# First products of four token quads at 512 tokens wide, in an attention and feed-forward kernel on one core

## The chip, the cores and the metric

The kernel runs on one core of a Trainium2 chip. The metric is device time in microseconds for one execution. The engines are TensorE (PE, with PEld for its weight loads), VectorE (DVE), ScalarE (ACT), GpSimd (POOL) and SyncE (SP). The last two mostly issue DMAs here.

## The reference

A gated recurrent attention over 4 batches, 8 heads, 768 tokens and 48 values a head is followed by a feed-forward layer of width 2048 on the 3072 tokens of 384 values. Cut to what matters:

```
for t in range(S):
    new_re = ar * S_re - ai * S_im
    new_im = ar * S_im + ai * S_re
    S_re, S_im = new_re + k[t] v[t]^T, new_im
    y[t] = q[t] S_re
x = y as (3072, 384)
h = x @ w_in
out = (h * sigmoid(h)) @ w_out
```

## The kernel before, in words

**Tiling.** The tokens are cut into 24 chunks of 128 (number n) and 12 pairs of chunks, 256 tokens each (number p). A chunk goes through gates, a phase and a decay (cumulative sums done as products with a triangle, tiles `phase` and `L`, lines 462 and 465), sine and cosine, rotated keys and queries (`kr`, `qr`), the weights `a` of the attention (line 609), their mask (`w`, line 620) and the output `y` (lines 639 and 642, for the first chunks 671 and 674). `put` (step x, lines 683 and 687) copies `y` from PSUM to `xT`; the last 16 values of three pairs of heads take a DMA (`third_of`, step xd, line 651).

**Feed-forward.** The first product makes 2048 hidden units in eight steps jp of 2 x 128 units. `hidden` (step h) writes one PSUM tile of 128 x 512 for pair p and step jp: two units blocks (ji) times 256 tokens. For the pairs 0 and 1 it is a plain float32 product (line 761). For the pairs from 2 on it is a sum of three float32r products: `xT` is split by `x_head`, `x_tail` and `x_diff` (steps xh, xt, xg) into the forms `xH` (ACT, line 778), `xL` (DVE, line 858) and `xD` (DVE, line 862), 128 x 768 each, and `w_in` into a head, a tail (`fine`, loaded again by DMA) and a difference (`mixed`). `sums` runs 3 forms x 3 parts of the 384 inputs x 2 units blocks = 18 products with 128 x 128 stationary weights and 256 moving tokens (line 768). `silu` (step g, line 312) makes `g`; `g_rounded`, `g_tail` and `g_diff` (steps gr, gb, gc; ACT line 914, DVE lines 858 and 862) split it into `head`, `tail` and `gd`, one buffer each; `result_of_parts` (step r, line 953) adds 12 products of 384 columns to the two PSUM tiles `o` of the pair. After eight steps `copied` (step oc, line 966) takes them out.

**Quads.** From pair 2 on, two neighbouring pairs (2 and 3, 4 and 5, and so on) share the loaded weights: the steps h, g, gr, gb, gc and r of an even pair p and of p + 1 stand close to each other for the same jp. Each pair has its own `xH`, `xL`, `xD`, in tiles with the tags of p % 2, so the forms of pair p + 2 wait only for the last product of pair p.

**Order.** The order of all instructions is written out by hand as a table of 1899 steps under `manual_schedule`: every engine runs its own instructions in the order in which the steps name them. The step `warm` puts idle products (bf16, 256 columns, line 990) on PE. The special functions of ACT lie in several tables; a step that needs another table than the loaded one puts an ACT_TABLE_LOAD in front (line 306).

Of the kernel before, what the change touches and what calls it, by code (L numbers as in the profile page):

```python
# [70 lines left out]
def kernel(  # L71
# [854 lines left out]
    def result(p, jp):  # L926
        if "o" not in A[p]:
            A[p]["o"] = o_tiles(p, 2)
# [3 lines left out]
        for m in range(2):  # L932
            for ji in range(2):
# [143 lines left out]
    with tc.manual_schedule():  # L1077
        for x in """
                re:0 im:0 e0:0 re:1g e1:0 e2:0 q:0g e3:0 im:2g im:1 e4:0 e0:1 hold: e1:1 re:2g e6:0
                e2:1 im:3g re:3g e5:0 k:0g F: v:0g e7:0 e4:1 e8:0 e6:1 F: L:0 e3:1 exp:0 e7:1 e8:1  # L1080
# [3 lines left out]
                R: dk:1 G8:1 G4:1 T:0.1 G6:1 ends:0 warm:20 T:0.2 G9:1 v:1g sm:0 H: q:2g lk:0 F:
                trig:1 dq:1 lk:1 last:0 T:0.0 F: J: v:2g Ga:1 s:0 rq:1.1 re:4g w:0.0 rk:1.1 R: L:2
                L:3 H: R: thirds:0 re:5g phase:2 S:0 t:1.1 rq:1.0 im:4g J: w:0.1 im:5g exp:2 rk:1.0
                k:3g ends:1 exp:3 t:1.2 m:0.0 rd:2 R: F: turn:2 t:1.0 trig:2 T:1.1 m:0.1 t:1.3 dk:2
                last:2 T:1.0 T:1.2 y:0 dq:2 T:1.3 phase:3 q:3g rd:3 thirds:1 rq:2.0 w:1.0 t:2.2
                ends:2 H: rq:2.1 x:0 J: w:1.1 G0:2 rk:2.0 turn:3 trig:3 dk:3 m:1.0 t:2.0 rk:2.1
                G5:2 dq:3 F: s:1 t:2.3 m:1.1 q:4g H: F: F: T:2.3 v:4g S:1 thirds:2 rk:3.1 G8:2 y:1  # L1090
                k:4g R: T:2.2 J: t:2.1 s:2 ends:3 rq:3.1 G1:2 last:3 thirds:3 x:1 rq:3.0 rk:3.0
                G7:2 t:3.1 J: T:2.0 H: R: S:2 h:0.0 H: G2:2 T:2.1 H: R: w:2.0 t:3.3 G3:2 m:2.0 J:
                G6:2 R: J: t:3.0 T:3.1 F: F: w:2.1 R: T:3.3 G4:2 t:3.2 G9:2 k:5g h:0.1 m:2.1 last:1
                q:5g w:3.1 H: T:3.2 T:3.0 y:2 m:3.1 R: Ga:2 x:2 im:6g w:3.0 L:4 exp:4 m:3.0 y:3 F:
                H: J: H: im:7g F: re:6g g:0.0 J: s:3 h:0.3 x:3 carried:4 dk:4 J: phase:4 R: F: S:3
                F: carried:5 R: g:0.1 H: R: h:0.2 rd:4 J: re:7g J: ends:4 turn:4 H: F: L:5 g:0.3
                r:0.0 dq:4 phase:5 k:6g h:1.1 trig:4 g:0.2 K:4 Q:4 R: tk:4 J: H: exp:5 G0:3 F:
                h:1.0 G5:3 J: G1:3 q:6g tq:4 H: last:4 F: H: v:5g G7:3 s:4 R: ends:5 F: G2:3 G8:3
                G3:3 r:0.1 J: rd:5 r:0.2 S:4 G6:3 H: G4:3 turn:5 G9:3 Ga:3 dq:5 R: g:1.0 td:4 g:1.1
                J: F: im:8g F: sm:2 last:5 H: trig:5 carried:6 dk:5 r:0.3 R: J: L:6 h:1.2 R: K:5  # L1100
                g:1.2 F: w:4.1 h:0.4 carried:7 tk:5 F: Q:5 H: J: lk:2 re:8g exp:6 H: h:1.3 R:
                phase:6 m:4.1 g:0.4 dk:6 R: rd:6 J: tq:5 R: turn:6 trig:6 phase:7 r:1.0 H: F: re:9g
                R: im:9g ends:6 s:5 r:1.1 k:7g J: last:6 rd:7 R: S:5 turn:7 H: trig:7 J: H: L:7
                w:4.0 F: m:4.0 G0:4 h:1.4 g:1.3 G5:4 h:1.5 dq:6 r:0.4 K:6 H: Q:6 R: J: g:1.4 F:
                G1:4 H: J: td:5 exp:7 q:7g R: ends:7 J: G7:4 y:4 G2:4 tk:6 tq:6 G3:4 r:1.2 G4:4
                G6:4 g:1.5 F: R: h:0.5 F: h:0.7 k:8 H: J: hl:8 R: g:0.5 H: J: J: G8:4 vh:1 vh:0
                G9:4 h:0.6 v:6g w:5.1 wq:0 x:4 vt:0 q:8 vt:1 wq:3 dq:7 td:6 wq:6 Q:7 m:5.1 dk:7
                w:5.0 s:6 r:1.3 Ga:4 ul:8 vh:2 vh:3 m:5.0 vk:0 L:8 ss:6 vk:1 q:9 k:9 wq:2 wq:4 K:7
                exp:8 y:5 carried:8 vt:2 im:10 g:0.6 vt:3 re:10 last:7 tk:7 vk:2 x:5 v:7g ht:8
                r:1.4 w:6.1 tq:7 dk:8 ut:8 w:6.0 m:6.1 carried:9 m:6.0 vk:3 phase:8 vh:4 g:0.7 vh:5  # L1110
                wq:7 ends:8 rd:8 vt:5 vt:4 td:7 turn:8 ht:9 ut:9 s:7 h:1.6 vk:5 ss:7 phase:9 h:1.7
                vh:6 vt:6 trig:8 vh:7 r:0.5 dq:8 im:11 Q:8 vk:4 hl:9 r:1.5 last:8 xd:2 wq:5 K:8
                ul:9 vk:6 y:6 vt:7 wq:1 wd:0 sd:7 rd:9 vk:7 x:6 re:11 wd:1 ws:0 wd:2 turn:9 wk:0
                w:7.0 wd:3 w:7.1 ws:2 wd:4 m:7.0 sd:6 m:7.1 G0:5 ws:4 wk:2 ws:3 y:7 tk:8 g:1.6 x:7
                wk:4 G5:5 v:8 last:9 wk:3 tq:8 L:9 g:1.7 xd:3 xh:2 wd:5 G1:5 r:1.6 xt:2 r:0.6 ws:5
                G7:5 lv:2.0 wk:5 r:0.7 r:1.7 ws:1 xg:2 G2:5 wd:6 wk:1 G3:5 wd:7 vx:2.0 ws:7 exp:9
                xh:3 xt:3 xg:3 G6:5 td:8 h:2.0 h:3.0 w:8.0 dk:9 ws:6 wk:7 s:8 lv:2.1 of:1 g:2.0
                m:8.0 wk:6 gr:2.0 G9:5 g:3.0 G8:5 w:8.1 Ga:5 vx:2.1 carried:10 re:12 of:0 gb:2.0
# [276 lines left out]
```

## Time and profile before

| what | value |
|---|---|
| median of 3 runs | 616.13 us (613.35 to 617.29) |
| profiled execution | 616.33 us |
| its span, first to last instruction | 614.5 us |
| mean granted clock of TensorE | 0.992 |
| busy: PE, DVE, ACT, POOL | 584.0, 495.9, 434.0, 222.4 us |

Durations below are from the profiled execution. It ran 1.8 us beyond its span and is within 0.2 us of the median. A matmul row of the profile lasts longer than the distance to the next one, because matmuls are pipelined; what one costs is read from start to start.

### The profile page before, as it was taken

How to read it: one execution, taken by the hardware profiler on the slowest of the kernel's cores; microseconds unless marked ns; L12 is line 12 of the kernel's file. 1: busy time of each engine (PE TensorE's matmuls, PEld its weight loads, DVE VectorE, ACT ScalarE, POOL GpSimd, SP SyncE). 2: the span in 40 equal slices, each digit the busy share in tenths (PEclk: the TensorE clock that was granted, in tenths of full speed). 3: DMA queues.
4: the chain of work that ended last, by engine and by line, in shares of the span. 5: the costliest groups of instructions: out<-in, count | busy, mean ns of one | idle time of the engine just before them, and what ended most of it. 6: DMA issues, size and time to landing. Idle time of an engine off the chain costs nothing. (4 is left out here: it accounts for less than half of the span.)

```text
span 614.5 us, 12718 instructions
## 1 busy us (share of the span) xinstructions
PE 584.0 (95%) x4404; PEld 538.2 (88%) x4404; DVE 495.9 (81%) x765; ACT 434.0 (71%) x689; POOL 222.4 (36%) x389
## 2 busy tenths in 40 slices
PE   3678999999998999999999999999999999999997
PEld 2457877777768999999999999999999999999996
DVE  5689989889988899888798989889989686566453
ACT  7789989799496798598797596897984742333222
POOL 6256343543631345533272553325640233000000
PEclk9879999999999999999999999999999999999999
DMA  9859698987778989768967768786768576664462
GB/s 180 201 136 190 184 195 189 203 160 205 202 234 244 218 163 238 161 157 186 212 159 186 154 156 225 180 187 149 177 156 255 146 186 155 203 201 136 160 201 80
DMA packets 167733, 112.30 MB, mean 183 GB/s; under 512 B 137725, under 2 KB 143425, under 8 KB 167665
## 3 DMA queue, kind: packets, MB, share of 16 engines
q1 hardware_dynamic: 151920, 89.69, 57.0%
q0 software_dynamic: 12288, 17.23, 14.0%
q10 hardware_dynamic: 3456, 4.52, 2.0%
q8 instruction: 36, 0.59, 0.4%
q14 instruction: 33, 0.26, 0.1%
HBM read 81.14 MB, written 11.47 MB: 151 GB/s over the span
## 5 line engine op out<-in xcount | busy, mean ns | idle before, releaser
L596 POOL DMA_DIRECT2D T<-sq x120 | 69.9, 590 | 67.3 <-PE h L768 24.0
L914 ACT ACTIVATE head<-g 128x512 fp32r<-128x512 f32 x75 | 47.4, 632 | 56.1 <-PE o L953 47.1
L312 ACT ACTIVATE g<-h 128x512 f32<-128x512 f32 x96 | 56.2, 593 | 40.5 <-PE h L768 34.4
L768 PE MATMUL h<-xL,fine 128*128 128x256 f32 x480 | 83.7, 283 | 0.8 <-DMA fine<-w_firsts 0.8
L768 PE MATMUL h<-xD,mixed 128*128 128x256 f32 x480 | 82.8, 280 | 1.0 <-DVE mixed L862 0.6
L306 ACT ACT_TABLE_LOAD x63 | 80.8, 1283 | 2.3 <-ACT ot L966 0.8
L858 DVE SCALAR_TENSOR_TENSOR tail<-g,head 128x512 fp32r<-128x512 f32 x75 | 51.5, 687 | 31.3 <-ACT head L914 21.6
L527 POOL DMA_DIRECT2D dec<-ends x48 | 31.3, 663 | 106.7 <-DMA ends<-eq 99.2
L768 PEld LDWEIGHTS h<-xD,mixed 128*128 128x128 f32 x480 | 68.5, 189 | 1.6 <-DVE mixed L862 1.0
L768 PEld LDWEIGHTS h<-xL,fine 128*128 128x128 f32 x480 | 68.3, 188 | 1.1 <-DMA fine<-w_firsts 1.1
L953 PE MATMUL o<-coarse,head 128*128 128x384 f32 x300 | 66.8, 344 | 0.0
L953 PE MATMUL o<-diff,gd 128*128 128x384 f32 x300 | 65.4, 339 | 0.7 <-DMA diff<-w_diffs 0.7
L768 PE MATMUL h<-xH,firsts 128*128 128x256 f32 x360 | 62.5, 282 | 0.0
L609 PE MATMUL a<-T 96*128 96x128 f32 x384 | 52.8, 285 | 3.9 <-ACT T L601 3.9
L953 PE MATMUL o<-fine,tail 128*128 128x384 f32 x260 | 55.6, 336 | 0.0
L609 PEld LDWEIGHTS a<-T 96*128 96x128 f32 x384 | 49.9, 198 | 6.5 <-ACT T L601 4.9
L953 PEld LDWEIGHTS o<-diff,gd 128*128 128x128 f32 x300 | 53.6, 188 | 1.5 <-DVE w L620 1.0
L862 DVE TENSOR_TENSOR gd<-tail,g 128x512 fp32r<-128x512 f32 x75 | 51.4, 686 | 4.2 <-PE o L953 0.2
L768 PEld LDWEIGHTS h<-xH,firsts 128*128 128x128 f32 x360 | 52.7, 188 | 0.5 <-issue 0.4
L953 PEld LDWEIGHTS o<-coarse,head 128*128 128x128 f32 x300 | 50.2, 188 | 1.5 <-issue 1.3
L728 POOL DMA_DIRECT2D S<-ssq x84 | 46.9, 607 | 12.8 <-DVE ssq L717 6.7
L953 PEld LDWEIGHTS o<-fine,tail 128*128 128x128 f32 x260 | 46.2, 188 | 0.0
(159 smaller groups left out, 1283.8 us busy)
## 6 DMA issues: line engine op xcount, KB each, us to landing
fine<-w_firsts SPq DMA_DIRECT2D x40, 384.0 KB
diff<-w_diffs SPq DMA_DIRECT2D x40, 384.0 KB
T<-sq SPq DMA_DIRECT2D x120, 64.0 KB
T<-sq POOLq DMA_DIRECT2D x120, 64.0 KB, 3.8
small<-in_moe_w_in_dram SPq DMA_DIRECT2D x16, 384.0 KB
raw<-in_moe_w_out_dram SPq DMA_DIRECT2D x16, 384.0 KB
small<-in_moe_w_out_dram SPq DMA_DIRECT2D x16, 384.0 KB
raw<-in_moe_w_in_dram SPq DMA_DIRECT2D x24, 192.0 KB
```

What stands on the lines that cost most here:

```text
L306: nc.scalar.preload_act_table_set(SETS[of][0])
L312: nc.scalar.activation(out=out, in_=in_, func=func, **kw)
L527: nc.gpsimd.dma_start(out=x["dec"][a * D:(a + 1) * D], in_=ends[n].rearrange("(h d) -> d h", d=D))
L596: (nc.gpsimd if a % 2 else nc.sync).dma_start(out=to[ts(b, Q), :, a], in_=X[n]["sq"][ts(a, Q), b].rearrange("p w h x -> p (w h) x"))
L609: nc.tensor.matmul(ps[:, h], lhsT=x["kT"][hh * HH + h], rhs=x["qT"][hh * HH + h], start=True, stop=True)
L728: (nc.gpsimd if g % 2 else nc.sync).dma_start(out=to[ts(b, Q), r, :, e], in_=sq[ts(g, Q), :, b, 0:e.stop - e.start])
L768: nc.tensor.matmul(ps[:, ji], lhsT=w(dc, ji), rhs=x[:, dc], start=(f == 0 and dc == 0), stop=(f == len(forms) - 1 and dc == ND - 1))
L858: nc.vector.scalar_tensor_tensor(out=dst, in0=whole, scalar=MORE / FINER, in1=head.bitcast(F32), op0=ALU.mult, op1=ALU.subtract)
L862: nc.vector.tensor_tensor(out=dst, in0=tail, in1=whole, op=ALU.subtract)
L914: nc.scalar.mul(g_form(p, jp, "head"), A[p]["g", jp], MORE * SPLIT / FINER)
L953: nc.tensor.matmul(to, lhsT=left[:, ji, ts(m, C)], rhs=right(ji), start=(first_ and ji == 0 and n == 0), stop=(last_ and ji == 1 and n == 2))
```

## The change: what it does

For the eight pairs 2 to 9 (`wide`), one step h no longer makes two units blocks for 256 tokens but one units block for the 512 tokens of both pairs: the step of the even pair makes block 0 of jp, that of the odd pair block 1. It is 9 products with 512 moving tokens in the place of 18 with 256. For this the forms of both pairs of a quad lie in one tile (`quad_tile`), which is written again only when the whole quad's products have been done; the pairs 10 and 11 use the same tiles but keep the narrow product. The small tiles of the start that borrow the room of the forms (`l0`, `l1`, `kr1`, `kr3`, four masks) are cut from these larger tiles.

The second product follows: `g`, `head`, `tail` and `gd` of a step now hold one units block for 512 tokens, and `result_of_quads` adds it to the four `o` tiles of both pairs. It has 12 products of 384 columns a step, as before.

The table of steps holds the same 1899 steps, the three `warm` among them, in another order.

```diff
@@ hidden
             fine, diff = (A[lead(p)][name, jp] for name in ("fine1", "mixed1"))
+            if wide(p):
+                forms = [(J[kind, lead(p)], w) for kind, w in
+                         (("xH", head_of(lead(p), jp)), ("xL", fine), ("xD", diff))]
+                for f, (x, w) in enumerate(forms):
+                    for dc in range(ND):
+                        nc.tensor.matmul(ps, lhsT=w[:, dc, ts(p % 2, C)], rhs=x[:, :, dc],
+                                         start=(f == 0 and dc == 0),
+                                         stop=(f == len(forms) - 1 and dc == ND - 1))
+                return
...
+    def wide(p):
+        return QUADS <= p < NP - 2
+
+    def quad_tile(key, i, dtype, name):
+        both = J.setdefault(key, None)
+        if both is None:
+            both = J[key] = moe.tile([C, 2, ND, T], dtype, tag=key[0], name=name, bufs=1)
+        return both[:, i]
+
+    def x_form(p, kind):
+        return quad_tile((kind, p - p % 2), p % 2, F32R, f"{kind}{p}")
...
     def x_head(p):
-        t = A[p]["xH"] = moe.tile([C, ND, T], F32R, tag=f"xH{p % 2}", name=f"xH{p}", bufs=1)
+        t = A[p]["xH"] = x_form(p, "xH")
         nc.scalar.mul(t, A[p]["xT"], MORE * SPLIT / FINER)
...
+    def result_of_quads(p, jp):
+        x, both = A[p], (lead(p), lead(p) + 1)
...
+        forms = ((x["head", jp], W["coarse"][:, jp * 2 + p % 2]),
+                 (x["tail", jp], W["fine", jp][:, p % 2]),
+                 (x["gd", jp], y["diff", jp][:, p % 2]))
+        for n, (left, right) in enumerate(forms):
+            for i, q_ in enumerate(both):
+                for m in range(2):
+                    nc.tensor.matmul(A[q_]["o"][m].rearrange("p n c -> p (n c)"),
+                                     lhsT=left[:, i, ts(m, C)], rhs=right,
+                                     start=(first_ and n == 0), stop=(last_ and n == 2))
...
-                at:0.0 warm:30 e5:1 F: dk:0 G0:1 k:1g an:0.0 dq:0 G5:1 phase:0 rd:0 R: turn:0
+                an:0.0 at:0.1 an:0.1 warm:34 phase:0 im:3g G0:1 rd:0 dk:0 turn:0 F: q:0g R: G8:1
```

The first place is PE at the first product of the first quad (pairs 2 and 3, jp 0). Before, two steps of 18 products:

```order
L768 MATMUL h2_0_1883<-xH2_1810,first0_1410 128x256 x3
L768 MATMUL h2_0_1883<-xL2_1822,fine2_0_1831 128x256 x3
L768 MATMUL h2_0_1883<-xD2_1844,mixed_1693 128x256 x3
L768 MATMUL h2_0_1883<-xH2_1810,first0_1410 128x256 x3
L768 MATMUL h2_0_1883<-xL2_1822,fine2_0_1831 128x256 x3
L768 MATMUL h2_0_1883<-xD2_1844,mixed_1693 128x256 x3
L768 MATMUL h3_0_1902<-xH3_1863,first0_1410 128x256 x3
L768 MATMUL h3_0_1902<-xL3_1865,fine2_0_1831 128x256 x3
```

Now two steps of 9, and the first of them reads the forms of both pairs (the tile is named after the first that was written to it):

```order
L766 MATMUL h2_0_1873<-xH2_1692,first0_1361 128x512 x3
L766 MATMUL h2_0_1873<-xL2_1840,fine2_0_1818 128x512 x3
L766 MATMUL h2_0_1873<-xD2_1851,mixed_1645 128x512 x3
L766 MATMUL h3_0_1902<-xH2_1692,first0_1361 128x512 x3
L766 MATMUL h3_0_1902<-xL2_1840,fine2_0_1818 128x512 x3
L766 MATMUL h3_0_1902<-xD2_1851,mixed_1645 128x512 x3
```

The number of products of these steps halves, and their moving side doubles.

The second place is ACT between the copy of the last output of pair 5 (`xT5` from `y11`) and the head form of that pair (`xH`). `s` and `mag` are gate steps, `eq` and `L` the decay of chunk 13. Before:

```order
L683 COPY xT5_2889<-y11_3057 128x3x128
L687 COPY y3_5_2891<-y11_3057 112x128
L914 ACTIVATE head3_7_3098<-g3_7_3011 128x512
L312 ACTIVATE s27_2981<-s1_7_2980 128x768
L312 ACTIVATE s27_2981<-s27_2981,one_b_106 128x768
L312 ACTIVATE s27_2981<-s27_2981 128x768
L312 ACTIVATE eq13_3107<-L13_3103 128x384
L312 ACTIVATE L13_3106<-L13_3103 128x384
L778 ACTIVATE xH5_3135<-xT5_2889 128x768
```

Now:

```order
L689 COPY xT5_2779<-y11_2864 128x3x128
L693 COPY y3_5_2781<-y11_2864 112x128
L944 ACTIVATE head2_7_2926<-g2_7_2825 128x512
L313 ACTIVATE s27_2811<-s1_7_2810 128x768
L313 ACTIVATE s27_2811<-s27_2811,one_b_106 128x768
L313 ACTIVATE s27_2811<-s27_2811 128x768
L944 ACTIVATE head3_7_2956<-g3_7_2821 128x512
L313 ACTIVATE eq13_2964<-L13_2911 128x384
L313 ACTIVATE L13_2963<-L13_2911 128x384
L313 ACTIVATE mag7_2914<-mag7_2914 128x768 x2
L808 ACTIVATE xH4_2850<-xT5_2779 128x768
```

One more head and two gate steps (`mag7`) stand ahead of the form now.

The third place is DVE at the start, where `th0`, the angle that the first phase sums, is made, and `k0` is decayed. Before:

```order
L394 TENSOR_TENSOR l0_124<-l0_124,s20_127 128x384
L540 TENSOR_TENSOR k0_158<-k0_158,L0_182 128x384
L433 SCALAR_TENSOR_TENSOR mag0_141<-re0_119,mag0_141 128x384
L435 SCALAR_TENSOR_TENSOR th0_128<-mag0_141,re0_119 128x384
L540 TENSOR_TENSOR q0_135<-q0_135,eq0_183 128x384
```

Now:

```order
L419 TENSOR_TENSOR mag0_139<-mag0_139,im0_121 128x384
L434 SCALAR_TENSOR_TENSOR mag0_139<-re0_119,mag0_139 128x384
L436 SCALAR_TENSOR_TENSOR th0_130<-mag0_139,re0_119 128x384
L434 SCALAR_TENSOR_TENSOR mag0_139<-re0_119,mag0_139 128x384
L436 SCALAR_TENSOR_TENSOR th0_130<-mag0_139,re0_119 128x384
L541 TENSOR_TENSOR k0_145<-k0_145,L0_170 128x384
```

The angles of both chunks stand ahead of the product with `k0` now; before, `k0` came first.

## Rows read from the trace of the kernel before

**Rows 1.** The page: busy time by engine, and the granted clock in 40 slices.

```profile
PE 584.0 (95%) x4404; PEld 538.2 (88%) x4404; DVE 495.9 (81%) x765; ACT 434.0 (71%) x689; POOL 222.4 (36%) x389
...
PEclk9879999999999999999999999999999999999999
```

**Rows 2.** Stretches: length, busy us of PE, PEld, DVE, ACT, POOL, clock, DMA.

```profile
0.00:20.00 20.00, 5.90 (x32) 3.98 (x32) 8.82 (x20) 14.39 (x23) 10.36 (x24) 1.00 0.93 182
20.00:40.00 20.00, 13.71 (x95) 10.87 (x96) 17.63 (x31) 17.11 (x27) 10.00 (x16) 0.87 0.67 184
300.00:320.00 20.00, 20.00 (x176) 19.63 (x176) 17.85 (x28) 18.04 (x29) 9.32 (x18) 1.00 0.77 170
```

**Rows 3.** Waits of PE, longest first: us in total, times, longest.

```profile
PE L L462 <- DVE l L394: 10.6, 1, 10.6
PE phase L462 <- DVE th L435: 4.1, 1, 4.1
...
PE tp L578 <- ACT L L312: 2.7, 1, 2.7
```

**Rows 4.** Timeline of PE: start us, length, instructions; a run of each kind of product.

```profile
66.19 2.76 PE L761 MATMUL h<-xT,w 128*128 128x256 f32 x12
...
68.79 1.06 PE L609 MATMUL a<-T 96*128 96x128 f32 x8
...
306.15 0.52 PE L768 MATMUL h<-xH,firsts 128*128 128x256 f32 x3
...
310.40 0.52 PE L465 MATMUL L<-l_parts,half_r 128*128 128x384 f32 x2
...
331.25 0.85 PE L953 MATMUL o<-coarse,head 128*128 128x384 f32 x4
...
333.35 0.51 PE L465 MATMUL L<-l_parts,half_r 128*128 128x384 f32 x2
```

**Rows 5.** Timeline of the start, all engines, with the idle time in front.

```profile
17.01 0.84 ACT L312 ACTIVATE s<-re 128x768 f32<-128x768 f32 x1 [1.07 <-DMA re<-in_a_re_dram]
...
18.90 0.56 DVE L540 TENSOR_TENSOR k<-k,L 128x384 f32<-128x384 f32 x1 [3.75 <-DMA k<-in_k_dram]
...
21.95 0.58 ACT L312 ACTIVATE turn<-phase,round_b 128x384 f32<-128x384 f32 x1 [2.64 <-PE phase L462]
...
59.89 0.46 ACT L683 COPY xT<-y 128x384 f32<-128x384 f32 x1
```

**Rows 6.** Timeline around pair 5's forms, all engines.

```profile
271.41 0.96 PE L953 MATMUL o<-coarse,head 128*128 128x384 f32 x4
271.51 0.48 ACT L683 COPY xT<-y 128x384 f32<-128x384 f32 x1 [0.86 <-PE y L642]
...
276.09 1.10 PE L609 MATMUL a<-T 96*128 96x128 f32 x8
276.27 0.84 ACT L778 ACTIVATE xH<-xT 128x768 fp32r<-128x768 f32 x1
276.94 0.97 PE L953 MATMUL o<-coarse,head 128*128 128x384 f32 x4
...
278.14 0.96 DVE L862 TENSOR_TENSOR xD<-xL,xT 128x768 fp32r<-128x768 f32 x1
...
280.00 0.60 PE L768 MATMUL h<-xH,first 128*128 128x256 f32 x3
```

**Rows 7.** ACT by line and form: count, busy us, mean ns, idle before.

```profile
L306 ACT ACT_TABLE_LOAD x63 | 80.8, 1283 | 2.3 <-ACT ot L966 0.8 <-ACT ot L960 0.4
...
L914 ACT ACTIVATE head<-g 128x512 fp32r<-128x512 f32 x75 | 47.4, 632 | 56.1 <-PE o L953 47.1 <-DVE w L620 3.5 <-issue 2.4
...
L312 ACT ACTIVATE mag<-mag 128x768 f32<-128x768 f32 x33 | 27.8, 842 | 0.9 <-ACT ot L966 0.4
...
L247 ACT ACTIVATE r<-raw 128x384 int32<-128x384 uint32 x16 | 8.7, 557 | 0.0
L601 ACT COPY T<-tp 96x512 f32<-96x512 f32 x16 | 8.7, 574 | 0.0
```

More of the change, by code (lines that the diff above doesn't have):

```diff
@@ L122 @@
     STREAM = 3
+    J = {}
     consts = ctx.enter_context(tc.tile_pool(name="consts", bufs=1))
@@ L926, in result @@
     def result(p, jp):
+        if wide(p):
+            result_of_quads(p, jp)
+            return
         if "o" not in A[p]:
@@ L1084 @@
[L1084 to L1118, printed above, removed]
-                h:2.1 lw:2.0 gc:2.0 h:3.1 r:2.0 carried:11 trig:9 lv:2.2 m:8.1 ss:8 ends:9 G4:5
@@ new lines @@
+                q:1g v:0g R: ends:0 trig:0 G5:1 L:1 rk:0.0 sm:1 J: G1:1 dq:0 rq:0.0 exp:1 rk:0.1
+                s:0 F: H: rq:0.1 G7:1 lk:1 F: k:1g phase:1 dq:1 G2:1 rd:1 G4:1 sm:0 H: H: v:1g lk:0
+                thirds:0 J: G3:1 last:0 warm:30 L:2 R: R: G6:1 exp:2 t:0.0 F: turn:1 G9:1 dk:1 q:2g
+                trig:1 T:0.0 S:0 t:0.2 T:0.2 L:3 re:4g Ga:1 k:2g t:0.1 ends:1 exp:3 F: warm:20
+                t:0.3 rk:1.0 rq:1.1 rk:1.1 phase:2 rd:2 t:1.0 T:0.1 t:1.3 T:1.0 R: T:0.3 H: dq:2
+                w:0.0 turn:2 J: trig:2 t:1.1 F: re:5g rq:1.0 H: dk:2 s:1 phase:3 w:0.1 J: F: t:1.2
@@ new lines @@
+                dk:5 G9:3 g:1.0 last:5 Ga:3 J: F: L:6 H: R: R: r:0.3 r:1.0 w:4.1 dq:5 F: carried:6
+                h:0.4 trig:5 J: K:5 Q:5 g:1.1 exp:6 g:0.4 H: sm:2 phase:6 rd:6 F: m:4.1 H: h:1.2 J:
+                R: carried:7 s:5 F: lk:2 H: H: H: im:8g re:8g R: im:9g R: h:1.3 turn:6 J: re:9g L:7
+                last:6 S:5 q:6g tk:5 g:1.2 dk:6 F: trig:6 phase:7 R: J: tq:5 J: F: ends:6 G0:4 J:
+                K:6 dq:6 Q:6 r:1.1 rd:7 G5:4 h:1.4 k:8 g:1.3 exp:7 h:1.5 F: R: H: R: H: J: td:5 H:
@@ new lines @@
+                L:9 xd:3 xh:3 xt:2 r:0.7 ws:7 wk:5 ws:4 xg:2 xt:3 vx:2.0 xg:3 r:1.7 td:8 h:2.0
+                exp:9 G3:5 wk:7 G6:5 dk:9 wk:4 G4:5 of:1 G9:5 h:3.0 g:3.0 s:8 ws:1 w:8.0 g:2.0
+                gr:2.0 lv:2.1 Ga:5 vx:2.1 h:2.1 h:3.1 carried:10 wk:1 gb:2.0 gc:2.0 v:9 of:0 K:9
+                lw:2.0 re:12 g:2.1 ss:8 ws:6 ht:10 carried:11 m:8.0 r:2.0 gr:3.0 ends:9 tk:9 s:9
+                ut:10 phase:10 hl:10 gb:3.0 lv:2.2 last:9 sm:3 gc:3.0 ul:10 ss:9 r:3.0 vx:2.2 dq:9
+                wk:6 re:13 L:10 rd:10 k:10 gr:2.1 lw:2.1 Q:9 ht:11 turn:10 g:3.1 gb:2.1 lv:2.3
@@ new lines @@
+                Q:15 G9:8 G4:8 r:5.3 gr:4.4 lw:4.4 Ga:8 gb:4.4 lv:4.6 hl:16 h:5.5 w:14.1 x:13
+                gc:4.4 q:16 m:14.1 ul:16 g:5.4 carried:16 r:4.4 L:16 gr:5.4 sm:6 gb:5.4 K:15 g:5.5
+                w:14.0 xd:6 q:17 exp:16 ht:16 lk:7 carried:17 lk:6 h:4.5 gc:5.4 im:18 k:16 ut:16
+                r:5.4 phase:16 tk:15 vx:4.6 tq:15 g:4.5 m:14.0 last:15 h:4.6 gr:4.5 S:12 ht:17
+                rd:16 g:4.6 turn:16 ut:17 trig:16 im:19 gb:4.5 dk:16 s:15 ends:16 re:18 h:5.6
+                gc:4.5 phase:17 lw:4.5 hl:17 lv:4.7 ul:17 ss:15 r:4.5 gr:5.5 re:19 gb:5.5 y:14
```

249 lines of the change are left out of this document (138 added, 111 removed).

## Prediction

> **What bounds the kernel now.** I read the page first. PE is busy 584.0 of 614.5 us, DVE 495.9 and ACT 434.0, and the clock is granted in full in nearly every slice [rows 1]. The reader is to see that PE is the bound and that its clock is not what is missing. The stretches say where the other 30.5 us are: PE is busy 5.90 of the first 20 us and 13.71 of the next, and 20.00 of 20 in a stretch of the middle, where DVE has 17.85 and ACT 18.04 [rows 2]. So after the start, time goes only if PE's own work shrinks, and it comes back wherever PE has to wait; DVE and ACT have some 2 us in 20 to spare, so a wait is made easily. The waits of PE are nearly all in the start: 10.6 us for `l`, 4.1 for `th`, 2.7 for a decay in front of the transposes [rows 3]. The timelines then give the price of one product [rows 4], the start [rows 5], and the chain that makes the forms of a pair [rows 6].
>
> The sum is made against the profiled execution, 616.33 us (span 614.5 and 1.8 around it), which lies 0.2 us over the median of the runs.
>
> **Part 1: the wide products.** Eight pairs times eight steps times 18 products are 1152; they become 576 with 512 columns. What one costs is read from start to start. Narrow: twelve runs of three, 306.15 to 310.40 us, so 4.25 us / 36 = 118.1 ns. The second product, 384 columns of the same kind: 331.25 to 333.35, so 2.10 us / 12 = 175.0 ns. Plain float32 products of 256 columns: 66.19 to 68.79, so 2.60 us / 12 = 216.7 ns a record [rows 4]. No row shows 512 columns. From 256 to 384 columns the price grows by 56.9 ns for 128, so I estimate 175.0 + 56.9 = 231.9 ns. Two narrow ones cost 236.2. The gain is 4.3 ns x 576 = 2.5 us. The bounds: at the narrow price per column nothing is gained (236.2); a loss is unlikely, since the price per column falls from 0.461 to 0.456 ns between the two widths. At the price of the longest record that the trace has for one load of weights, 216.7 ns, the gain is 19.5 x 576 = 11.2 us. I take 2.5, because the 384-column row is of the same kind of product and the float32 one is not, and I keep 0 and 11.2 for the range.
>
> The second product keeps its count (12 of 384 columns a step), its buffers and the order head, tail, difference, so it costs the same. So do silu and the splitting of `g`: as many elements in as many instructions.
>
> **Part 2: the start of a quad.** This is the edit with a price. Before, the first step of a quad needed only the forms of the even pair; it ran while those of the odd pair were made. Now it needs both. In the trace of pair 5 the last output ends at 271.41, ACT copies it from 271.51, `xH` ends at 276.27 + 0.84 = 277.11, `xD` at 279.10, and pair 5's first product starts at 280.00 without a wait: the chain takes 7.7 us and PE had 8.6 us of other work [rows 6]. In the new order PE has, between the last output of the odd pair and the first wide product: for quad 4 three steps r, two steps w and one sum `L`. A step r is 2.10 us, a step w 0.85 (276.09 to 276.94), `L` 0.35 (333.35 is followed by the next products at that distance, two records of 0.175), together 6.3 + 1.7 + 0.35 = 8.35 us. For quad 6 it has one r more, 10.45; for quad 8, 8.35. The cover is still there.
>
> The chain is longer, though. ACT needed 5.6 us from copy to end of `xH` (271.51 to 277.11). Quad 4: one more head (0.63) and two gate steps (2 x 0.842) stand in front [rows 7], so 5.6 + 2.3 = 7.9; with 2.0 us for `xL` and `xD` and 0.1 in front of the copy it is 10.0, and PE waits 1.65 us. Quad 6: without the three gate steps (2.6), but with three table loads, one gate step, one silu (taken as a head's 0.63) and three heads in the place of one (3.85 + 0.84 + 0.63 + 1.26 = 6.6), 9.6 + 2.1 = 11.7, a wait of 1.2. Quad 8: without the gates, with one table load, one head and three sines (1.28 + 0.63 + 1.7, the sines taken at 0.557, a step of that width) 6.6 + 2.1 = 8.7, a wait of 0.35. Quad 2 had both pairs' forms in front of its first product before too, so nothing. Sum: 3.2 us lost. The bounds are 0 (ACT reaches the copy with time in hand) and some 12 (rival 3). Behind a first product that waits, PE's whole queue stands, and ACT's next silu waits for it.
>
> The one tile for both pairs also lets the first form of a new quad wait for the last product of both pairs. On PE that product is followed by 13 us of other work before the next wide one in quad 4 (four r, four w, the last output), so this costs nothing; the wait lies under those.
>
> The new order has six more table loads, 6 x 1.283 = 7.7 us on ACT [rows 7]. ACT idles 47.1 us in front of the heads alone, waiting for PE [rows 7], and this hides them, where they are not already in the sums above.
>
> **Part 3: the start.** DVE's product with `k0` stood in front of the first angle and waited 3.75 us for its load; the phase on PE and `turn` on ACT (2.64 us) waited behind it. ACT also waited 1.07 us for `re` [rows 5]. Now the angles come first, and one block of weights less is loaded ahead of them, so both waits on ACT may go: 3.7 us. Up to the second copy into `xT`, at 59.89, behind which the first product of the feed-forward stands, ACT has one more copy of `T` (0.57) and two more `r` (2 x 0.557) [rows 7]: 1.7 us. Net 2.0 us gained. What PE has done by then is the same but for one transposition and one `a` more and one `s` less, about even. The idle products stay 84 in number and lie again in front of waits, so they are priced at nothing; if one of the three stands in front of ready work, 34 of 256 columns cost 3.6 us at 2.4 GHz, an estimate. The bounds of this part are a loss of 2 (all 1.7 paid, no wait gone) and a gain of 6.8 (rival 2).
>
> **Sum.** 616.33 - 2.5 + 3.2 - 2.0 = 615.0 us for the profiled execution, and 0.2 less for the median of runs: 614.8 us. This is within what measuring this kernel can tell from no change, about 1% or 6.2 us.
>
> **Rivals.**
> 1. *The wide product runs at the price of the float32 record.* The gain is 11.2 in the place of 2.5: 606.1 us. For it: the 11 ns that a narrow product takes beyond its columns at 2.4 GHz (106.7 ns) could be paid once a product. Against it: at 384 columns the surplus is 15 ns (175.0 - 160), so it grows with the columns. The Trainium skill, page "TensorE: Matmul & The Clock Gate", section "Wait — 56ns, not 53.3ns?", puts a warm product at its columns by 2.4 GHz plus about 2.5 ns, 215.7 ns at 512; by this the gain would be 20.5 x 576 = 11.8 us, but by this rule the rows would read 109 and 162 ns, and they read 118.1 and 175.0.
> 2. *The start moves up whole.* PE's waits for `th` and for the decay, 4.1 and 2.7 us [rows 3], both go, and ACT's 1.7 us are hidden: 6.8 in the place of 2.0, so 610.0 us. For it: the waits are in the trace. Against it: ACT and DVE are busy 17 of 20 us from 20 us on [rows 2], so what PE does not wait for here it waits for later.
> 3. *Slower: the quad's start has no cover.* The last result in the cover needs its own head, tail and difference, and the same ACT and DVE queues make them. If these come due in front of the forms, each quad start loses a head, a tail, a difference and the result behind them, 0.63 + 0.7 + 0.7 + 2.10 = 4.1 us, at three quads 12.3: 627.1 us. It decides from some 2.5 us more at each. For it: ACT is busy 18 of 20 us in the middle [rows 2]. Against it: in pair 5's chain ACT still idled 0.86 us in front of the copy [rows 6].
> 4. *The change doesn't do what it says:* 512 columns cost two times 256. Then 614.8 + 2.5 = 617.3 us. For it: from 256 to 384 columns the price per column falls by 1% only [rows 4]. Against it: it does fall.
>
> **How the numbers follow.** The forecast has 0.44 (its own range 611 to 619), rival 1 0.20, rival 2 0.10, rival 4 0.12, rival 3 0.14. Faster by over 1% (below 610.0) are rival 1, half of rival 2 and 0.04 of the forecast: 0.29. Slower by over 1% (above 622.3) is rival 3: 0.14. The rest, 0.57, is within 1%. The range 605 to 621 leaves out rival 3 and the lower end of rival 1.
>
> **What would show it.** The wide products start 232 ns apart; 217 would make rival 1 right, 236 rival 4. PE's waits show rows for `xD` or `xH` in front of the first wide product at three places, 0.3 to 2 us each; 4 us each would make rival 3 right. The wait for `th` shrinks and the second copy into `xT` of the first pair lies near 58 us; near 53 would speak for rival 2. Past 622 the forecast is wrong, and below 610 too.

## The result, and the profile after

The changed kernel takes 608.46 us (median of 5 runs, 608.15 to 609.22) beside 616.13 us (5 runs, 613.35 to 617.29) for the kernel before: ratio 0.9889, with a 95% interval from 0.9860 to 0.9918. The forecast was 614.8, within 1% of the kernel before. The kernel is faster by 1.1% and lies 6.3 us below the forecast: inside the range of 605 to 621, but outside the forecast's own 611 to 619, and below the 610 that the prediction named as the sign that the forecast is wrong. Its profiled execution took 608.15 us with a span of 606.4, so 8.2 us less than the profiled execution of before.

From the page of the changed kernel, the lines that answer to [rows 1] and to the first two of [rows 7]:

```profile
PE 580.6 (96%) x3828; PEld 507.4 (84%) x3828; DVE 495.6 (82%) x765; ACT 441.2 (73%) x695; POOL 224.2 (37%) x389
...
PEclk9799999999999999999999999999999999999999
...
L307 ACT ACT_TABLE_LOAD x69 | 88.5, 1283 | 2.3 <-ACT ot L1017 0.8
...
L944 ACT ACTIVATE head<-g 128x512 fp32r<-128x512 f32 x75 | 47.2, 629 | 47.9 <-PE o L986 27.6
```

576 products fewer, six table loads more, and the same mean clock (0.992). The waits of PE, longest first (answering to [rows 3]; total us, times, longest):

```profile
PE L L463 <- DVE l L395: 8.7, 1, 8.7
PE s L705 <- DVE kr L558: 5.3, 2, 4.0
PE phase L463 <- DVE th L436: 1.5, 1, 1.5
PE h L776 <- ACT xT L689: 1.5, 1, 1.5
```

No row for `xH` is there, and only one of 0.3 us for `xD`, in the first quad (179.39 us). The next rows are the timeline around the start of quad 4, all engines, answering to [rows 6]:

```profile
263.10 0.97 PE L986 MATMUL o<-coarse,head 128*128 128x384 f32 x4
263.21 0.48 ACT L689 COPY xT<-y 128x384 f32<-128x384 f32 x1 [0.57 <-PE y L648]
...
270.12 0.83 ACT L808 ACTIVATE xH<-xT 128x768 fp32r<-128x768 f32 x1
271.14 0.95 DVE L888 SCALAR_TENSOR_TENSOR xL<-xT,xH 128x768 fp32r<-128x768 f32 x1
271.80 0.86 PE L766 MATMUL h<-xH,first 128*128 128x512 f32 x3
272.12 0.96 DVE L892 TENSOR_TENSOR xD<-xL,xT 128x768 fp32r<-128x768 f32 x1
272.50 0.86 PE L766 MATMUL h<-xL,fine 128*128 128x512 f32 x3
273.20 0.90 PE L766 MATMUL h<-xD,mixed 128*128 128x512 f32 x3
```

Three wide products stand 0.70 us apart (271.80, 272.50, 273.20), some 233 ns each; over all pairs of neighbouring wide products the median distance is 232 ns. The last form `xD` ends at 273.08, 1.3 us after the unit has begun and 0.1 us before its own products come up. PE does not stop.

Where the 8.2 us went, from start times on PE in the two profiles: the first feed-forward product starts at 57.94 us in place of 60.40, which is 2.5 us. From there to the first product in parts it takes 119.3 us in place of 121.9, with nearly the same work between them (8 products `a` and 4 transpositions `tp` less and 16 products `s` more, by their starts 0.2 us less): 2.6 us. From there to PE's end it takes 424.6 in place of 427.8, 3.2 us; 2.3 of them are the wide products, priced at the median distances, and 0.9 is less waiting. The two starts, before:

```profile
60.40 2.86 PE L761 MATMUL h<-xT,w 128*128 128x256 f32 x12 [0.40 <-ACT xT L683]
...
182.28 0.82 PE L768 MATMUL h<-xH,first 128*128 128x256 f32 x3
```

and after:

```profile
57.94 2.86 PE L776 MATMUL h<-xT,w 128*128 128x256 f32 x12 [1.51 <-ACT xT L689]
...
177.25 1.15 PE L766 MATMUL h<-xH,first 128*128 128x512 f32 x3
```

### The profile page after: what moved, and what is told of

It reads as the page before. It is cut to its first block, busy times and chain, and to the rows that moved or that the text cites. A ratio compares the mean times of both kernels' runs of the same rounds, so it can differ in the third digit from the quotient of the medians.

```text
span 606.4 us, 11509 instructions
## 1 busy us (share of the span) xinstructions
PE 580.6 (96%) x3828; PEld 507.4 (84%) x3828; DVE 495.6 (82%) x765; ACT 441.2 (73%) x695; POOL 224.2 (37%) x389
## 5 line engine op out<-in xcount | busy, mean ns | idle before, releaser
L600 POOL DMA_DIRECT2D T<-sq x120 | 70.5, 612 | 31.9 <-PE a L613 10.8
L944 ACT ACTIVATE head<-g 128x512 fp32r<-128x512 f32 x75 | 47.2, 629 | 47.9 <-PE o L986 27.6
L986 PE MATMUL o<-coarse,head 128*128 128x384 f32 x256 | 57.1, 343 | 0.2 <-ACT ot L1017 0.2
L766 PE MATMUL h<-xL,fine 128*128 128x512 f32 x192 | 55.3, 396 | 0.8 <-DMA fine<-w_firsts 0.8
L766 PE MATMUL h<-xD,mixed 128*128 128x512 f32 x192 | 55.4, 396 | 0.5 <-DVE xD L892 0.3
L986 PE MATMUL o<-diff,gd 128*128 128x384 f32 x256 | 55.4, 337 | 0.0
L986 PEld LDWEIGHTS o<-diff,gd 128*128 128x128 f32 x256 | 45.4, 188 | 0.5 <-DVE w L626 0.3
L776 PE MATMUL h<-xT,w 128*128 128x256 f32 x192 | 43.7, 380 | 1.5 <-ACT xT L689 1.5
L766 PEld LDWEIGHTS h<-xD,mixed 128*128 128x128 f32 x192 | 35.7, 188 | 10.5 <-DVE xD L892 1.2
L766 PEld LDWEIGHTS h<-xL,fine 128*128 128x128 f32 x192 | 35.9, 188 | 9.9 <-DMA fine<-w_firsts 1.3
L968 PE MATMUL o<-w,g 128*128 128x384 f32 x128 | 43.5, 488 | 0.0
L766 PE MATMUL h<-xH,firsts 128*128 128x512 f32 x144 | 42.7, 405 | 0.0
```

Of the source, the lines that this page charges most:

```text
L600: (nc.gpsimd if a % 2 else nc.sync).dma_start(out=to[ts(b, Q), :, a], in_=X[n]["sq"][ts(a, Q), b].rearrange("p w h x -> p (w h) x"))
L766: nc.tensor.matmul(ps, lhsT=w[:, dc, ts(p % 2, C)], rhs=x[:, :, dc], start=(f == 0 and dc == 0), stop=(f == len(forms) - 1 and dc == ND - 1))
L776: nc.tensor.matmul(ps[:, ji], lhsT=of_first(w1, dc, jp * 2 + ji), rhs=A[p]["xT"][:, dc], start=(dc == 0), stop=(dc == ND - 1))
L944: nc.scalar.mul(g_form(p, jp, "head"), A[p]["g", jp], MORE * SPLIT / FINER)
L968: nc.tensor.matmul(A[p]["o"][m].rearrange("p n c -> p (n c)"), lhsT=A[p]["g", jp][:, ji, ts(m, C)], rhs=w2[jp][:, ji], start=(j == 0), sto ...
L986: nc.tensor.matmul(A[q_]["o"][m].rearrange("p n c -> p (n c)"), lhsT=left[:, i, ts(m, C)], rhs=right, start=(first_ and n == 0), stop=(las ...
```

## The experiments

Medians of the kernel before beside them were 615.7 to 617.3 us, depending on the chip. So ratios to it are given, and where the times of two chips are set against each other, the difference by the ratios stands beside.

**1. The changed kernel with narrow products.** Everything else, tiles and order, is as in the changed kernel.

```diff
-                for f, (x, w) in enumerate(forms):
-                    for dc in range(ND):
-                        nc.tensor.matmul(ps, lhsT=..., rhs=x[:, :, dc], ...)
+                for i in range(2):
+                    for f, (x, w) in enumerate(forms):
+                        for dc in range(ND):
+                            nc.tensor.matmul(ps[:, i], lhsT=..., rhs=x[:, i, dc], ...)
```

> Everything of the changed kernel (order, tiles, units blocks, second product) but each product of 512 tokens is made as two of 256 again, one per pair. Theory A (the width gives only its price per product, 232 in the place of 2 x 118 ns): 576 x 4.3 ns = 2.5 us slower than the changed kernel, about 611 us, products 118 ns apart. Rival B (the halved number of products and weight loads is what brought the 8 us): about 616 us. Rival C (the order alone brought them): 608.5 us.

Measured: 615.19 us (612.53 to 617.16), ratio 0.9974 (0.9950 to 0.9997). This is 6.7 us above the changed kernel (5.2 by the ratios), where the products alone explain 2.3. In this order the width is worth more than its products' price, by some 3 to 4 us. The time is nearest to rival B's 616; whether for B's reason is what experiment 5 tests. The longest wait of the narrow version behind its first 60 us lies in the first quad, all engines:

```profile
182.63 0.52 PE L769 MATMUL h<-xL,fine 128*128 128x256 f32 x3
...
184.49 0.32 SPq L875 DMA_DIRECT2D fine<-w_firsts  x1
...
187.87 0.62 PE L769 MATMUL h<-xL,fine 128*128 128x256 f32 x3 [1.67 <-DMA fine<-w_firsts]
```

and in the changed kernel:

```profile
180.90 0.86 PE L766 MATMUL h<-xL,fine 128*128 128x512 f32 x3
...
182.06 0.32 SPq L872 DMA_DIRECT2D fine<-w_firsts  x1
...
185.25 0.86 PE L766 MATMUL h<-xL,fine 128*128 128x512 f32 x3
```

The room of the streamed `fine` weights is free for the next load once its last products are done. The wide version has 4.35 us between the last use and the next (180.90 to 185.25) and the load fits in. The narrow one has 3.6 us (182.63 to 187.87, less the wait) and PE stands for 1.67. This place alone does not show the width, though: in two more profiles of the changed kernel the same product waits 0.44 us (experiment 8) and 1.15 (experiment 12), and in the kernel before 0.84; the profile shown here waits 0.85 for the next load, at 212.91.

Behind the wait of 1.67 us the granted clock of the narrow version fell to half for 3.4 us, which no profile of the changed kernel has there (the columns are those of [rows 2]):

```profile
188.70:192.10 3.40, 3.13 (x14) 3.13 (x15) 2.87 (x5) 0.17 (x1) 0.00 (x0) 0.50 1.02 299
```

That costs about as much as the wait, some 1.6 us, half of the 3.13 that the products took. Three waits for `mixed`, the difference of the weights, add 1.2 us; the profiles of the changed kernel have none above 0.15. The profile is of the slowest of the 12 runs, so how much of this a usual run has is not shown.

**2. The narrow kernel before, with the new order up to its first product in parts,** then its own order.

```diff
-                at:0.0 warm:30 e5:1 F: dk:0 G0:1 k:1g an:0.0 dq:0 G5:1 phase:0 rd:0 R: turn:0
+                an:0.0 at:0.1 an:0.1 warm:34 phase:0 im:3g G0:1 rd:0 dk:0 turn:0 F: q:0g R: G8:1
...
```

> The kernel before, narrow and with its own tiles, with the steps up to its first product in parts put in the order that the changed kernel has there; from there on the old order. Theory A (the start and the preparation of the weights bring 5.0 us, and PE keeps them because it is the bound): 616.1 - 5.0, about 611 us, first product in parts near 177 us. Rival D (what the start gains is waited away later): 614 to 616 us with the first product in parts near 177 us all the same.

Measured: 617.32 us (615.83 to 619.94), ratio 1.0030 (1.0012 to 1.0049). The first product in parts starts 4.8 us earlier than before (177.48), but the last first product of that quad starts at 266.15 in place of 266.18. The whole gain has been waited away by there. The waits of PE from 57 to 200 us begin with these:

```profile
PE a L609 <- DVE w L620: 4.1, 1, 4.1
PE h L761 <- ACT xT L683: 1.3, 1, 1.3
```

A wait of 4.1 us for a mask on DVE, which the kernel before does not have, takes the place of the gain, together with the granted clock, which stood at half from 187.4 to 194.2 us behind that wait:

```profile
187.00:195.00 8.00, 6.58 (x29) 5.92 (x30) 7.43 (x11) 2.09 (x5) 1.63 (x2) 0.57 0.71 215
```

The time lies a little above rival D's 614 to 616, and its reason is D's. Here a better start was worth nothing, since the order behind it did not take it up.

**3. The cover taken away.** In the changed kernel, the last second product ahead of quads 4, 6 and 8 is put behind the quad's first wide unit (and the copy of that result with it).

```diff
-... w:12.1 r:3.7 oc:3.1 xg:5 Ga:7 m:12.0 h:4.0 carried:14 ...
+... w:12.1 xg:5 Ga:7 m:12.0 h:4.0 r:3.7 oc:3.1 carried:14 ...
```

> The changed kernel with the last result of the quad before (12 products, 2.1 us) moved behind the first wide product of quads 4, 6 and 8. Theory A (a wide step takes xH, xL and xD one after another, 0.70 us apart, and has no more than 0.1 us to spare): PE waits about 2 us more at each of the three, up to 6 us in all, 612 to 614.5 us. Rival E (ACT makes the forms earlier when nothing else is waiting, so the cover was not needed): 608 to 609 us.

Measured: 618.66 us (614.49 to 620.29), ratio 1.0037 (1.0013 to 1.0061), 10 us above the changed kernel (9 by the ratios) and above theory A's 612 to 614.5. Of PE's waits, those that the changed kernel does not have, or has shorter:

```profile
PE o L986 <- ACT ot L1017: 2.9, 2, 2.0
...
PE a L613 <- ACT L L313: 1.7, 2, 1.1
...
PE h L766 <- ACT xH L808: 1.1, 1, 1.1
PE h L766 <- DVE xL L888: 1.0, 2, 0.8
```

One step r of 2.1 us moved at each of three places costs 10 us. Only 2.1 of it stands in front of the forms. More of it comes behind, where at quads 4 and 8 a second product waits 0.83 and 2.02 us until ACT has copied the old results out, which now end later.

**4. The price of a product by itself.** The changed kernel with 96 products added behind step g:9.7, 16 of each kind, whose sums nobody reads.

```diff
+        rows = [flat_[:, 0:w_] for w_ in (128, 256, 384, 512)] + [x[:, :, 0], half_x[:, 0:512]]
+        for i, rhs in enumerate(rows):
...
+            for _ in range(n):
+                nc.tensor.matmul(ps if i == 4 else to[:, 0:rhs.shape[1]], lhsT=left, rhs=rhs,
+                                 start=True, stop=True)
```

> The changed kernel with 96 idle products added behind the last silu of pair 9: 16 each of float32r with 128, 256, 384 and 512 neighbouring columns, 512 columns as the quads read them (two pieces of 256), and bf16 with 512. Theory A (a float32r product costs more than its columns, by an amount that grows with them): 59, 118, 174, 232, 232 and 216 ns apart. Rival F (the two pieces cost it): 216 for 512 neighbouring columns, 232 for the two pieces.

Measured, median from start to start: float32r 112 ns at 128 columns, 118 at 256, 173 at 384, 229 at 512, whether these lie in one piece or in two; bf16 216 at 512. One run took 626.1 us. So from 256 columns on a product costs what the two narrower forms said, as theory A has it, and two pieces cost nothing. At 128 columns theory A had 59 and is wrong. The Trainium skill, page "TensorE: Matmul & The Clock Gate", section "Wait — 56ns, not 53.3ns?", gives columns by 2.4 GHz plus about 2.5 ns, 215.7 ns at 512 columns. The bf16 row agrees with it, and no float32r row does.

**5. Narrow in the succession of the wide unit.** As experiment 1, but each form is used in one go: two products of 256 side by side with the same weights. The first and the last product of a unit stay wide.

```diff
+                        if (f, dc) in ((0, 0), (2, 2)):
+                            nc.tensor.matmul(ps, lhsT=..., rhs=x[:, :, dc], start=(f == 0), stop=(f == 2))
+                            continue
+                        for i in range(2):
+                            nc.tensor.matmul(ps[:, i], lhsT=..., rhs=x[:, i, dc], start=False, stop=False)
```

> After's order and tiles; of the nine wide products of a unit the first and the last stay 512 wide, the seven between are each split into two of 256 side by side, so that the three forms are used in the same succession, and at nearly the same moments, as in the changed kernel; nothing is left out. By their pitches alone 64 units x 7 x (2 x 118.1 - 232) ns = 1.9 us more work than the changed kernel: 610.4. Theory A, that the narrow version of the first experiment lost its further 4 us because it used each form twice, 0.35 us apart, and so needed the second and third form earlier and let go of the streamed weights later: 610 to 611.5. Rival B, that what cost was the doubled number of products and weight loads, whatever their succession: 613.5 to 615.5 (7/9 of the 6.7 us that the narrow version lost, 608.5 + 5.2 = 613.7, at the least).

Measured: 611.04 us (608.42 to 613.41), ratio 0.9926 (0.9899 to 0.9953). The changed kernel beside it took 608.98 us. The difference is 2.1 us where the products' price says 1.9, as theory A has it. So most of what experiment 1 lost beyond the price came from the succession, not from the number of products: using a form for both halves of the quad at once asks for the next form later and lets the streamed weights go earlier. How much of it are the waits themselves, and how much the half clock behind one of them, is not separated.

**6. The changed kernel's products in the order of before.** At the quads' starts the steps that must be are moved:

```diff
-... last:13 h:4.0 lv:4.1 gb:3.7 xh:5 ... r:3.7 xt:5 k:14 w:12.0 xg:5 ... r:4.0 ... oc:3.0 Ga:7 oc:3.1
+... last:13 lv:4.1 gb:3.7 xh:5 ... r:3.7 ... xt:5 k:14 w:12.0 xg:5 h:4.0 ... oc:3.0 oc:3.1 r:4.0 ...
```

> The changed kernel's code with the order of before; only at the quads' starts the first units stand behind the last form of the quad, and the copies of the quad before ahead of its first result, since the wide units need both. Nothing is left out. Theory A, separate terms: -2.3 us for the width, the old start unchanged, and at the three later quad starts the first unit behind forms that the old order makes as late as the narrow units allowed, some 1 us each: 615 to 617.5 beside a before of 616.1. Rival B, that the width brings the 6.7 us between the narrow version and the changed kernel in any order: 608.5 to 610.5. Rival C, that the old order's quad starts stall the wide units as the run without cover did (10 us): 619 to 625.

Measured: 624.90 us (624.05 to 625.98), ratio 1.0163 (1.0140 to 1.0186). With the order of before, the changed kernel's code is 9 us slower than the kernel before. The time is rival C's. Of PE's waits:

```profile
PE o L986 <- ACT ot L1017: 3.4, 5, 1.3
...
PE o L986 <- DVE gd L892: 1.9, 1, 1.9
PE o L986 <- DMA diff<-w_diffs: 1.6, 1, 1.6
```

The time is lost mostly around the quads' starts, but at the results and outputs there, not in front of the wide products, so the place is not rival C's: of 8.6 us of waits behind 200 us only one, of 0.15 us for `xH` at 464.53, stands in front of a quad's first wide product. Behind one of the waits the granted clock fell too (last section). First products of the quads come 4.7, 7.3 and 9.1 us later than before (278.66, 369.81, 464.53). How much of the 9 us the moved copies and forms bring, and how much the width itself, is not separated here, since the width cannot be had without them.

**7. The changed kernel with the steps ahead of its first feed-forward product in the old order.**

```diff
-                an:0.0 at:0.1 an:0.1 warm:34 phase:0 im:3g G0:1 rd:0 dk:0 turn:0 F: q:0g R: G8:1
+                at:0.0 warm:30 e5:1 F: dk:0 G0:1 k:1g an:0.0 dq:0 G5:1 phase:0 rd:0 R: turn:0
...
```

> The changed kernel with the steps ahead of its first feed-forward product put back in the order in which before has them; all behind is the changed kernel's. Nothing is left out. First feed-forward product near 60.4 in place of 57.94. Theory A, that the start's 2.46 us come through to the end: 610.5 to 611.5. Rival B, that they are waited away later, as with the old rest of the order in the second experiment: 608 to 609.3. Rival C, that steps between the first feed-forward product and the first one in parts come late too, and the 2.6 us of waiting that went there return: 612.5 to 614.

Measured: 613.22 us (612.01 to 617.77), ratio 0.9974 (0.9953 to 0.9995), 4.2 us above the changed kernel on the same chip. From PE's timeline:

```profile
39.30 2.07 PE L613 MATMUL a<-T 96*128 96x128 f32 x8 [3.00 <-ACT T L605]
...
60.74 1.19 PE L613 MATMUL a<-T 96*128 96x128 f32 x8 [2.70 <-ACT T L605]
...
63.43 1.06 PE L776 MATMUL h<-xT,w 128*128 128x256 f32 x2
```

The total is what rival C gave, but not for its reason: the first feed-forward product already comes at 63.43, 3 us later than the 60.40 I named. The steps ahead of it are the new table's, in the old one's succession; with the old table's own steps, in experiment 6, it comes at 58.74. So this start is not quite the old one, and why it is slower was not pursued; the wait of 2.70 us at 60.74, which the kernel before does not have, is most of it. Behind it nothing returns. To the first product in parts it takes 119.9 us, as in the new order. The 4.4 us by which this product comes later than in the changed kernel beside it (59.08) go through to the end, and theory A's mechanism holds with the new order behind.

**8. The changed kernel again,** beside 5, 6 and 7, with no edit.

> The changed kernel itself, beside the three others on the same chip. 607.9 to 609.2; if it stands elsewhere, the others are read against it.

Measured: 608.98 us (607.66 to 609.55), ratio 0.9898 (0.9877 to 0.9918). In this profile the first feed-forward product starts at 59.08.

**9. The last form first.** The first wide unit of quads 4, 6 and 8 uses `xD`, then `xL`, then `xH`.

```diff
+                if p in (4, 6, 8) and jp == 0:
+                    forms = forms[::-1]
```

> After's order and code, but the first wide unit of quads 4, 6 and 8 uses its three forms the other way round: xD first, xL next, xH last. Nothing is left out. Theory A, that a quad's start waits for each form only when its own products come up, and that this is why the three starts cost nothing where I counted the wait to the end of xD: PE now waits at these units for the end of xD, which in the changed kernel's profile came 1.28, 0.99 and 1.41 us after the first products had started (273.08 against 271.80, 362.27 against 361.28, 452.23 against 450.82), together 3.7 us, so 612 to 613, with rows of h waiting for xD of 1 to 1.5 us at each of the three. Rival B, that the lost time is made up behind the start, since the other engines run on: 608.5 to 610.

Measured: 612.54 us (610.81 to 614.00), ratio 0.9928 (0.9902 to 0.9954), 3.6 us above the 608.98 of experiment 8, and 0.003 of the time (1.8 us) by the ratios, whose intervals overlap; the kernel before took 617.31 us on this chip. The time is theory A's, and so are the waits. PE's timeline at the three starts:

```profile
273.81 0.97 PE L768 MATMUL h<-xD,mixed 128*128 128x512 f32 x3 [1.17 <-DVE xD L894]
...
364.39 0.97 PE L768 MATMUL h<-xD,mixed 128*128 128x512 f32 x3 [0.79 <-DVE xD L894]
...
455.76 0.97 PE L768 MATMUL h<-xD,mixed 128*128 128x512 f32 x3 [1.22 <-DVE xD L894]
```

Once the unit needs the last form first, waits of 1.17 + 0.79 + 1.22 = 3.2 us are there. That this is the sum that I had forecast for the quads' starts is partly chance, since I had it as 1.65, 1.2 and 0.35. The waits settle the failed step: they come when the last form is needed first, and are absent when it is needed last.

**10 and 11. No idle products.** The changed kernel without its three `warm` steps, run twice; **12** is the changed kernel beside the second.

```diff
-                an:0.0 at:0.1 an:0.1 warm:34 phase:0 im:3g G0:1 rd:0 dk:0 turn:0 F: q:0g R: G8:1
+                an:0.0 at:0.1 an:0.1 phase:0 im:3g G0:1 rd:0 dk:0 turn:0 F: q:0g R: G8:1
...
```

(and the same for `warm:30` and `warm:20`).

> The changed kernel without its three groups of idle products (84 products, 12.9 us of PE ahead of 38 us); nothing else is changed, and nothing that is computed is left out. Theory A, that they hold the clock: without them the granted clock stands at half over more of the first 60 us, and the first feed-forward product comes at 59 to 62 in place of 57.94: 609.5 to 613. Rival B, that the second and third group (4.9 and 2.4 us) stand in the way of products that are ready: 604.5 to 607. Rival C, that DVE and ACT set the start, and neither is seen: 608 to 609.3.

> The changed kernel without its 84 idle products, once more, beside the changed kernel itself on one chip. Theory A, that the start is set by DVE and ACT alone, so that slower products ahead of 37 us and faster ones are the same: within 1 us of the run beside it. Rival B, that the idle products of the second and third group stand in the way: 1 to 2 us below the run beside it.

> The changed kernel itself, as the other's neighbour. 607.9 to 609.2.

Measured: 607.46 us (605.40 to 610.01), ratio 0.9856 (0.9818 to 0.9894); then 606.18 us (605.17 to 609.13), ratio 0.9857 (0.9830 to 0.9883), beside 608.19 us (607.18 to 609.25), ratio 0.9881 (0.9857 to 0.9906), for the changed kernel. That is 2.0 us less on the same chip, at the upper end of what the second of these expectations gave rival B; the 607.46 lies between rivals B and C of the first. The two intervals of the same chip overlap, so a gain is likely but not certain. Start of PE's timeline without the idle products (experiment 11):

```profile
17.63 1.65 PE L463 MATMUL phase<-th,upto_r 128*128 128x384 f32 x2 [7.46 <-DVE th L436]
...
30.05 1.62 PE L463 MATMUL L<-l,half_r 128*128 128x384 f32 x2 [1.57 <-DVE l L413]
31.46 1.06 PE L582 MATMUL tp<-ident,kr 128*96 128x128 f32 x4
```

and with them (experiment 12):

```profile
17.64 0.91 PE L463 MATMUL phase<-th,upto_r 128*128 128x384 f32 x2 [1.83 <-DVE th L436]
...
28.89 4.45 PE L1041 MATMUL idle<-upto_r 128*128 128x256 bf16 x30
33.18 0.81 PE L463 MATMUL L<-l,half_r 128*128 128x384 f32 x2
33.82 0.60 PE L582 MATMUL tp<-ident,kr 128*96 128x128 f32 x4
```

With the idle products what follows them runs in half the time. But the second group stands in front of an `L` whose input is there: without the group it starts 3.1 us earlier (30.05 against 33.18), and the first feed-forward product comes at 56.70 in place of 58.65. This version is faster than the kernel before; against the changed kernel a gain is likely.

## Why the prediction was right and wrong

*The bound.* PE as the bound, with a full clock, held behind the start. In the first 60 us the granted clock stood at half for 10.2 us in the profile before and for 6.8 in the profile after, which the prediction did not weigh.

*Part 1, the product.* Right, and not by luck: 231.9 ns forecast, 232 measured, and 2.3 of 2.5 us; experiment 4 finds the same step from 256 to 384 to 512 columns. What this part left out is that the width changes the succession of forms. I priced the edit as products and took its waits from the rest. Experiments 1 and 5 show, in the new order, some 3 us that come from using each form for both pairs at once (3.7 by the times, 2.5 by the ratios). How much of that is in the gain over the kernel before is not shown: behind the first product in parts its waiting was only 0.9 us longer.

*Part 2, the start of a quad: the step that failed.* I forecast that "PE waits 1.65 us" at quad 4, 1.2 at quad 6 and 0.35 at quad 8, and the three starts cost nothing. The chain was right at quad 4: from the end of the last output at 263.10 to the end of `xD` at 273.08 it took the forecast 10.0 us, and the cover was 8.7 where I had 8.35. At quad 6 it took 11.8 where I had 11.7, under a cover of 10.8; at quad 8 it took 9.9 where I had 8.7, under 8.5. So `xD` ended 1.28, 0.99 and 1.41 us behind the start of the unit. The comparison was wrong. I set the cover against the end of the last form, but the unit begins with `xH`, 2.1 us before that, and comes to `xL` 0.70 and to `xD` 1.40 us later. Each form was there when its turn came, `xD` with 0.1 to 0.5 us to spare, and experiment 9 brings the wait back by turning the turns round. With 1.40 us allowed for `xD`, the forecast's own chain and cover give waits of 0.25, 0 and 0. This accounts for 3.2 of the 6.3 us.

*The table loads* at nothing: nothing speaks against it. ACT's idle time in front of the heads is 47.9 us in place of 56.1, and the part of it that ends with a product of PE 45.0 (27.6 on line 986, 17.4 on line 1004) in place of 47.1, so there was room; no run has the loads by themselves.

*Part 3, the start.* 2.0 us forecast for the first feed-forward product; 2.5 in the profile after, 1.3 and 1.75 in the profiles of experiments 8 and 12. Right in size; the cause is open. Of the two waits on ACT that I let go, the 2.64 us for `turn` are gone and 0.41 of the 1.07 us for `re` are left. But experiment 6, with the old order of the start, comes at 58.74, 1.7 us before the 60.40 of the kernel before, and in the profile before the granted clock was at half from 38.1 to 44.9 us, where it is full after. From 40 to 50 us, before and after:

```profile
40.00:50.00 10.00, 10.00 (x63) 7.26 (x62) 7.58 (x17) 8.09 (x15) 6.14 (x10) 0.76 0.50 126
...
40.00:50.00 10.00, 8.88 (x74) 7.96 (x75) 9.23 (x19) 9.94 (x20) 6.52 (x12) 1.00 0.83 172
```

So how much of this gain belongs to the order is not shown. The idle products "priced at nothing" were probably wrong in the changed kernel: one group stands in front of ready work, the case that I had named, and all three together cost some 2 us, if the gain of experiment 11 is real. The kernel before has 84 of them too, and what they cost there was not measured.

*The term that was missing.* From the first feed-forward product to the first in parts PE has nearly equal work in both kernels and takes 2.6 us less. It is the order of the steps there, since it goes with the order whatever the width: 121.9 us with the old order (before) and 122.0 (experiment 6), 119.8 with the new one and narrow products (experiment 2), 119.9 with the old start (experiment 7), 119.3 to 119.6 in three profiles of the changed kernel. I had looked at the three places of the order that I could price and took the rest for equal. The kernel before has four rows of waits of 0.3 to 0.5 us there, 1.5 together, and the changed kernel has none; 0.2 is the work that moved ahead of this stretch, and the other 0.9 was not traced. With the 3.2 of part 2 this is 5.8 of the 6.3 us.

*The rivals.* Rival 1 is out: 232 ns, and 216 for bf16 alone. Rival 2 is out: the start moved by 1.3 to 2.5 us, not 6.8. Rival 4 is out by the product's price. Rival 3 is out for the changed kernel. That a quad's start without cover is dear is real: 618.66 us in experiment 3. But there and in experiment 6 PE waited mostly for copies, forms, decays, masks and streamed weights, and only once, for 1.9 us, for the difference of a result, which is what rival 3 priced; that 624.90 lies near its 627.1 is chance.

*The parts together.* Ratios to before: new order and narrow products 0.9974, old order and wide products 1.0163, both 0.9889. The parts do not add up: -0.3% and +1.6% make -1.1%. The new order wins next to nothing with narrow products, the wide products lose in the old order (with the steps that they force to move), and my sum had each with a value of its own.

## What to carry to other kernels

A unit of work that reads several operands in turn waits for each at its own turn: set each one's arrival against its own first use, not the last arrival against the first use. When products are made wider, look at what the new succession asks for later and lets go of earlier; in the new order here that was worth at least as much as the cheaper products. A wide unit and the order around it are one change: price the pair, since either half alone can come out at nothing or at a loss.

## What was not expected of the hardware

A float32r product of 128 columns with a weight load of its own took 112 ns, hardly less than one of 256 (118): below 256 columns narrowing bought almost nothing (experiment 4).

At 17.63 us in experiment 11 two products of 384 columns last 1.65 us where they last 0.91 behind the idle products, and the granted clock of the stretch reads full (the columns are those of [rows 2]):

```profile
8.00:20.00 12.00, 3.99 (x6) 1.67 (x6) 8.67 (x19) 10.28 (x19) 3.88 (x7) 1.00 1.03 203
```

PE had run only two products before, at 8.55 us, and then waited 7.46 us. The first record of the clock in this trace is a rise to full at 33.8 us; four transpositions take 1.06 us at 31.46 and 0.60 at 34.13. So the column alone does not tell at which rate the products of a start run; their durations do.

In experiment 6 PE waited 1.92 us for `gd` at 265.4 us, and behind it the granted clock fell to half from 268.7 to 272.1 (0.66 in the row below), in which 32 products of the output took 3.6 us:

```profile
268.00:273.00 5.00, 4.69 (x38) 4.10 (x37) 3.59 (x5) 1.60 (x4) 0.00 (x0) 0.66 0.39 60
```

At full clock the same products stand 55 ns apart, 1.8 us for 32. A wait in the middle can so cost about as much again as its own row says. The same stands behind the waits of 1.67 us in experiment 1 and 4.13 us in experiment 2. It does not follow every wait: behind one of 2.02 us, at 469.27 in experiment 3, the clock stayed full.
